# Moving the last recurrent groups of two batches behind the MLP's 64-feature products

## The chip, the cores and the metric

One core of a Trainium2 chip runs the whole kernel. The metric is the device time of one execution in microseconds. The kernel before took 391.72 us (median of three runs, 391.14 to 392.08). Engines are called as in the profile: PE (TensorE, matmuls), PEld (its weight loads), DVE (VectorE), ACT (ScalarE), POOL (GpSimd), SP (which issues the DMAs).

## The reference

An mLSTM cell over 4 batches, 8 heads, 768 tokens and a head size of 40 is followed by a Fourier mix with an MLP on the 320 features of each token. Cut to what is computed:

```
for t in range(S):                                   # mLSTM, per batch and head
    m_new  = max(f[t] + m, i[t])
    f_stab, i_stab = exp(f[t] + m - m_new), exp(i[t] - m_new)
    C = f_stab * C + i_stab * outer(v[t], k[t])
    n = f_stab * n + i_stab * k[t]
    y[t] = sigmoid(o[t]) * (C @ q[t]) / max(abs(n @ q[t]), 1)
x  = y as (batch, 768, 320)
u  = x + real(fft(fft(x, axis=1), axis=2))
un = (u - mean(u)) / sqrt(var(u) + 1e-6)
out = u + relu(un @ w_ch1) @ w_ch2                   # w_ch1 320x1280, w_ch2 1280x320
```

## The kernel before

Batches are counted from 1 to 4 in the text (0 to 3 in the code), chunks of 128 tokens from 0 to 5. A batch passes three stages: the recurrence (mLSTM), the mix (two Fourier steps as matmuls over folded tokens), and the MLP. The stages of neighbouring batches are interleaved: while TensorE works on the MLP of one batch, the recurrence of the next runs between its matmuls.

The order is written out by hand. `at(slot, phase, fn, ...)` puts a step into a plan; `run` calls the steps sorted by slot and then by phase (EVAC 0, FILL 1, MAIN 2, FILL_PE 3), and each engine executes its instructions in the order in which they were issued. An engine that waits for a semaphore holds up all that stands behind it in its queue.

**The recurrence of batches 2 to 4** (`plan_halves`, L762) takes each chunk in halves of 64 tokens, with 64-row and 64-column matmuls. Chunk c has a start slot s, before always three slots after the last. Steps at s: scores (L626) and the new state (L637) on TensorE, exponentials on ScalarE (L491, four at slot s-1 and four at s), decay, scaling and mask on GpSimd (L652, L507, L501, L515), state adds and weighing on DVE (L667, L672). Three slots later comes the output: the part from the state (L674), the part from the chunk in two turns (L685), between which ScalarE reads one element (`halves_between`, L699) so that the second turn waits for the first, and a tanh (L605). All these matmuls have line L519. The output tile `ph` is a single one (`heads`), as are the scores. One slot later `mlstm_finish` (L712 to L720, five DVE operations) reads `ph` and writes the chunk's x; the chunks 0, 1 and 3 run backwards in time order and are then moved by DMAs (`halves_rows`, L728). For the last chunk (`end`) the state part and the first turn stand ahead of the slot's MLP step, the second turn behind it.

**The mix** folds pairs of chunks on DVE (`mix_fold`, L815 to L827, pairs (2,3), (1,4), (0,5) at slots x_done), then the folded rows once more in three steps (`mix_fold_again`, L844 to L854).

**The MLP of batches 2 to 4** (`plan_mlp`, L1271) computes its first layer in five blocks of four slots. A block (`mlp_block`, L1111) multiplies by the first and the last 128 features in a scheme with seven products for eight; each product is a 128x128 by 128x384 matmul in fp32 (L1121). The 64 features between are four matmuls on 64 rows (`tails`, L1126), two at a time on the two halves of the array's rows. Product by product, with the lines of the operands:

- slot 0: in block 0 a first product B (`begin`, L1138, copied out by ScalarE, L1139); then A01 (L1146)
- slot 1: S2 (L1152, copied out, L1153, into h12) and A10 (L1151 or L1155, added to h12 by DVE, L1130)
- slot 2: S4 (L1160), S3 (L1161, copied out, L1162), then the four tails, and DVE adds three banks to the hidden values (L1165 to L1167, all in line L1130)
- slot 3: B of the next block, and T4 (L1172), with a relu on ScalarE (L1173)

The second tail adds into the bank that DVE's add of A10 has read; the fourth into the bank that ScalarE's copy of S3 (L1162) has read; B of the next block writes the bank that the first of DVE's three adds reads. The sums of inputs that the scheme needs are four DVE subtractions per batch (`mlp_sums`, L1109) just before block 0: A10 of block 0 reads the second one's result, S2 the third's. The second layer (`mlp_out_pair`, L1240) follows the blocks.

The MLP of batch 2 has its blocks at slots 63 to 82, that of batch 3 at 95 to 114. The recurrence of batch 3 starts at slot 53 and that of batch 4 at slot 83. In the line for the sixth argument of `plan_mix`, `done` holds the slots at which the folds become possible:

```
done = [s_mlstm + n for n in ((16, 19, 22) if b == 0 else (18, 21, 22))]
```

Of the kernel before, what the change touches and what calls it, by code (L numbers as in the profile page):

```python
# [53 lines left out]
def kernel(  # L54
# [33 lines left out]
    def bank(name, shape, n=None):  # L88

        return ps_m.tile(shape, FP, name=name, tag=f"pm{next(turn) if n is None else n}")  # L90
# [33 lines left out]
    def at(slot, phase, fn, *args):  # L124
        plan.setdefault((slot, phase), []).append((fn, args))
# [7 lines left out]
    EVAC, FILL, MAIN, FILL_PE = range(4)  # L133
# [625 lines left out]
            at(t, FILL_PE + (2.5 if c < 4 else 1), mlstm_turn, b, c, c < 4)  # L759
            at(x, FILL + 0.05, mlstm_finish, b, c)  # L760

    def plan_halves(b, s0, stride=3):  # L762
        for c in range(NT):
            s = s0 + stride * c
            t = 22 + 2 * c if b == 1 and c < 3 else s - 5
            at(t, FILL, mlstm_load, b, c)
            at(t, FILL, mlstm_load_max, b, c)
            at(34 if b == 1 and c == 2 else t + 1, FILL, mlstm_load_decay, b, c)
            at(s - 1, FILL, mlstm_load_o, b, c)
            at(s - 1, FILL, mlstm_scale_v, b, c)  # L770
            at(s - 1, FILL + 0.3, mlstm_exp, b, c, 0)
            at(s, FILL, mlstm_exp, b, c, NP)
            at(s, FILL_PE + 2.05, halves_scores, b, c)
            at(s, FILL_PE + 2.5, halves_to_state, b, c)
            for i in range(2):
                at(s + i, FILL + 0.05, halves_decay, b, c, i)
                at(s + 1 + i, FILL - 0.2, halves_add, b, c, i)
            at(s, FILL + 0.1, mlstm_scale_q, b, c)
            at(s + 1, FILL, mlstm_mask, b, c)
            if (b, c) == (3, 2):  # L780
                at(s + 2, MAIN + 0.1, halves_weigh, b, c)
            else:
                at(s + 1, FILL + 0.55 if b == 1 and c > 0 else MAIN + 0.7, halves_weigh, b, c)
            end = c == NT - 1
            at(s + 3, MAIN - 0.1 if end else FILL_PE, halves_from_state, b, c)
            at(s + 3, MAIN - 0.1 if end else FILL_PE, halves_from_chunk, b, c, 0)
            at(s + 3, MAIN if end else FILL_PE + 0.5, halves_between, b, c)
            at(s + 3, FILL_PE + 3, halves_from_chunk, b, c, 1)
            at(s + 3, FILL_PE + 0.6, mlstm_tanh, b, c)
            at(s + (5 if (b, c) == (2, 2) else 4), {(2, 4): FILL + 0.3, (3, 3): FILL - 0.3}.get((b, c), FILL + 0.3 if b == 1 else MAIN + 0.55), mlstm_finish, b, c)  # L790
            at(s + 6, FILL - 0.6, halves_rows, b, c)

# [215 lines left out]
    def plan_mix(b, s0, x_done, s_feat, s_add, s_turn):  # L1010
        for j in range(TG):
            p = TG - 1 - j
            at(x_done[j] + (b > 1 and j == TG - 1), FILL + 0.5 if b < 2 else FILL_PE + 0.2, mix_fold, b, p)
            if b == 0:
                at((s0 - 4, s0 - 2, s0)[j], FILL_PE + 4, mix_seq, b, p, (0, 1))
                at((s0 - 2, s0 - 2, s0)[j], FILL_PE + 4, mix_tail, b, p)
            elif b == 1 or j == 0:
                if b > 1:
                    for step, slot in enumerate((x_done[0], x_done[-1] + 2, x_done[-1] + 6)):
                        at(slot, FILL_PE + 0.25, mix_fold_again, b, step)  # L1020
                at(s0, FILL_PE + 4, mix_seq, b, p, (0,))
                at(s0 + 1, FILL_PE + 4, mix_seq, b, p, (1,))
                at(s0 + 2, FILL_PE + 4, mix_tail, b, p)
        for i in range(2):
            at(s0 + 1 if b == 0 else s0 + 1 + i, FILL, mix_seq_out, b, i)
        at(s0 + (1 if b == 0 else 3), FILL + 0.1, mix_tail_out, b)
        for p in range(TG):
            at(s_feat[p], FILL_PE + 4, mix_feat, b, p)
        for c, a, t in zip(ORDER, s_add, s_turn):
            at(a, FILL if b < 2 else MAIN - 0.3 if c == 0 else MAIN + 0.5, mix_add, b, c)  # L1030
            at(t, FILL + 0.1, mix_center, b, c)
            at(t, FILL_PE + (5 if b == 0 or c in ORDER[:4] else -0.1), mix_turn, b, c)
            if b > 0:
                at(t, FILL_PE + 6, mix_turn_out, b, c)
            elif t < s_mlp:
                at(t + 1, FILL + 0.2, mix_turn_out, b, c)
            else:
                at(t + 1, EVAC, mix_turn_out, b, c)
# [31 lines left out]
    def hidden(gr, f):  # L1070
        return hid[gr, f % 2][:, f // 2 * TG * L:(f // 2 + 1) * TG * L]
# [7 lines left out]
    def block(t, n):  # L1079
        return t[:, n * L:(n + 1) * L]  # L1080
# [20 lines left out]
    def mlp_u(gr, ch):  # L1101
        return uT_bufs[gr][:, ch].rearrange("p c t -> p (c t)")
# [8 lines left out]
    def mlp_block(b, i, step):  # L1111

        k = mixes[b]
        f = 2 * i
        T2, T3, T4 = w1x["T"]
        A = {(r, ch): block(w1_sb[:, ch], f + r) for r in range(2) for ch in range(2)}

        def product(bank, w, u, start=False):  # L1120
            nc.tensor.matmul(bank, w, u, start=start, stop=True, skip_group_check=True)  # L1121

        def tails(gr, banks):
            for r, bank in enumerate(banks):
                rows = slice(r * TAIL, (r + 1) * TAIL)
                nc.tensor.matmul(bank, block(w1t_sb, i)[rows], mlp_u(gr, 1)[rows], start=False, stop=True,  # L1126
                                 skip_group_check=True)

        def add(h, bank):
            nc.vector.tensor_tensor(out=h, in0=h, in1=bank, op=OP.add)  # L1130

        banks = list(range(4) if i % 2 else range(3, -1, -1))

        def begin(i):


            k.p1 = bank("pm", [L, TG * L], 0 if i % 2 else 3)
            product(k.p1, block(w1_sb[:, 0], 2 * i), mlp_u(0, 0), True)  # L1138
            nc.scalar.copy(out=hidden(0, 2 * i), in_=k.p1)  # L1139

        (h11, h21), (h12, h22) = ([hidden(gr, f + r) for r in range(2)] for gr in range(2))
        if step == 0:
            if i == 0:
                begin(0)
            k.pm = [k.p1, bank("pm", [L, TG * L], banks[1])]
            product(k.pm[1], A[0, 1], mlp_u(0, 2), True)  # L1146
        elif step == 1:
            k.pm.append(bank("pm", [L, TG * L], banks[2]))
            p1, _, p5 = k.pm
            if i == 0:  # L1150
                product(p5, A[1, 0], mlp_u(1, 0), True)  # L1151
            product(p1, block(w1x["S2"], i), T2)  # L1152
            nc.scalar.copy(out=h12, in_=p1)  # L1153
            if i > 0:
                product(p5, A[1, 0], mlp_u(1, 0), True)  # L1155
            add(h12, p5)
        elif step == 2:
            k.pm.append(bank("pm", [L, TG * L], banks[3]))
            p1, p2, p5, p3 = k.pm
            product(p3, block(w1x["S4"], i), mlp_u(1, 2), True)  # L1160
            product(p1, block(w1x["S3"], i), T3)  # L1161
            nc.scalar.copy(out=h22, in_=p1)  # L1162
            tails(1, (p3, p5))
            tails(0, (p2, p1))
            add(h12, p3)  # L1165
            add(h22, p5)
            add(h11, p2)  # L1167
        else:
            p1 = k.p1
            if i < NFF // 2 - 1:  # L1170
                begin(i + 1)
            product(p1, A[1, 1], T4)  # L1172
            nc.scalar.activation(out=h21, in_=p1, func=AF.Relu, scale=-1.0)  # L1173
# [97 lines left out]
    def plan_mlp(b, s):  # L1271
        groups = range(NT // TG)
        for i in range(NFF // 2) if b > 0 else ():
            for step in range(4):
                at(s, MAIN, mlp_block, b, i, step)
                s += 1
            end = i == NFF // 2 - 1
            for n, (gr, f) in enumerate(((1, 2 * i + 1), (1, 2 * i), (0, 2 * i))):
                at(*((s - 1, MAIN + (-0.1 if gr else 0.1)) if end else (s + n, MAIN + 0.5)), mlp_relu_in_place, gr, f)
# [31 lines left out]

    def plan_batch(b, s_mlstm, s_mix, s_mlp):
        (plan_halves if b > 0 else plan_mlstm)(b, s_mlstm)
        done = [s_mlstm + n for n in ((16, 19, 22) if b == 0 else (18, 21, 22))]
        assert s_mix >= done[-1] and s_mlp >= s_mix + 9
        late = [s_mlp + 2 * c for c in range(TG)]
        if b == 0:
# [13 lines left out]
        s = s_mlp + NFF + 2  # L1331
# [4 lines left out]

    s_mlp = 31
    plan_batch(0, 0, 22, s_mlp)
    plan_batch(1, 32, 54, s_mlp + MLP_SLOTS)
    plan_batch(2, 53, 83, s_mlp + 2 * MLP_SLOTS)  # L1340
    plan_batch(3, 83, 115, s_mlp + 3 * MLP_SLOTS)
    for n in range(4):
# [149 lines left out]
```

## Time and profile before

The profiled execution took 392.19 us, of which the span of the engines' work is 390.4 us.

| | us or count |
|---|---|
| profiled execution, its span | 392.19, 390.4 |
| median of the runs | 391.72 |
| ACT busy, POOL busy | 172.1 (44%), 134.9 (35%) |
| L519 groups of the recurrence, one whole group in the MLP | 1.9 us |
| L1126 MATMUL, mean of one | 508 ns |
| L1121 MATMUL, mean of one (two records a product) | 506 ns |
| L1130 DVE add of a bank, mean of one | 548 ns |
| mean granted clock of TensorE | 0.999 |

A line of the trace in order of time gives start, duration, engine, line, operation, the tiles written and read, and how many instructions are merged; in brackets stands how long the engine was idle before and who released it. As matmuls overlap in the pipe, distances from start to start say more than durations. A product of fp32 shows as two records. The chain of waits gives, in order of time, what the end depended on.

### The profile page before, as it was taken

The page shows a single profiled execution, that of the slowest core. Times are in us where ns is not written, and L with a number is a line of the kernel's source. Part 1 is how long each engine was busy: PE and PEld are TensorE (multiplying, and loading weights), DVE is VectorE, ACT ScalarE, POOL GpSimd, SP SyncE. Part 2 cuts the span into 40 slices and gives each one's busy share as a digit, 9 for nine tenths or more (in the row PEclk, how much of TensorE's full clock was granted, in tenths as well). Part 3 has the DMA queues.
Part 4 walks back from the last instruction along what each step waited for, and adds up shares of the span by engine and source line. Part 5 has one row for each costly group of instructions (what it writes and reads, how often), then busy time and mean ns, then how long its engine had stood idle before and what let it go on. Part 6 is the DMA issues. An engine that isn't in the chain of part 4 may idle for free.

```text
span 390.4 us, 10585 instructions
## 1 busy us (share of the span) xinstructions
PE 379.6 (97%) x4174; PEld 277.3 (71%) x4174; DVE 278.0 (71%) x671; ACT 172.1 (44%) x481; POOL 134.9 (35%) x237
## 2 busy tenths in 40 slices
PE   8999899999999999999999999999999999999996
PEld 6777555656667777765569998755588996556996
DVE  7789988499599587476975699777655785346652
ACT  6887357477543233655462314554530133545000
POOL 5739504467954442173254134541500000020000
PEclk9999999999999999999999999999999999999999
DMA  7887499579394345437700626400000000000101
GB/s 224 287 235 204 159 254 255 179 214 271 109 231 116 122 116 150 149 102 184 182 2 28 174 80 192 135 20 2 0 2 34 6 30 34 2 0 0 35 34 35
DMA packets 25631, 44.78 MB, mean 115 GB/s; under 512 B 5727, under 2 KB 14766, under 8 KB 25454
## 3 DMA queue, kind: packets, MB, share of 16 engines
q1 hardware_dynamic: 25582, 44.11, 38.9%
q8 instruction: 33, 0.54, 0.6%
q14 instruction: 16, 0.13, 0.1%
HBM read 38.49 MB, written 4.12 MB: 109 GB/s over the span
## 4 chain that ended last, share of the span: by engine, by line
PE 78%; DVE 14%; issue 3%; ACT 3%; POOL 1%; DVEq 0%; ACTq 0%; POOLq 0%
PE po L1240 20%; PE pm L1121 15%; PE po L1184 8%; PE pm L1059 7%; PE ph L519 4%; PE pm L1126 4%; PE pu L938 4%; PE ps L519 3%; PE pm L1050 2%; PE put L981 2%; PE pz L907 1%; PE pz L895 1%; DVE h L1130 1%; DVE so L716 1%; PE pM L221 1%
## 5 line engine op out<-in xcount | busy, mean ns | idle before, releaser
L1190 DVE SCALAR_TENSOR_TENSOR x<-po,rstd,x 128x160 f32<-128x160 f32 (+1 forms) x69 | 27.1, 394 | 37.4 <-PE po L1240 32.5
L1130 DVE TENSOR_TENSOR h<-h,pm 128x384 f32<-128x384 f32 x60 | 30.5, 548 | 27.1 <-PE pm L1121 12.6
L652 POOL TENSOR_TENSOR C<-C,decB 128x164 f32<-128x164 f32 x30 | 15.9, 531 | 67.5 <-DVE C L667 56.1
L1121 PE MATMUL pm<-uT,w_sb 128*128 128x384 f32 x90 | 37.7, 506 | 1.3 <-DVE uT L1109 0.6
L491 ACT ACTIVATE W<-W,colT 128x64 f32<-128x64 f32 x144 | 37.5, 339 | 0.4 <-DMA W<-M_d 0.4
L1184 PE MATMUL po<-w_sb,h 128*128 128x320 f32 x120 | 34.3, 435 | 0.0
L515 POOL TENSOR_SCALAR_AFFINE_SELECT W<-W 64x512 f32<-64x512 f32 x36 | 27.3, 759 | 10.6 <-ACT W L491 9.1
L1005 POOL TENSOR_TENSOR t<-rstd 128x6 f32<-128x6 f32 x12 | 3.3, 273 | 79.9 <-DVE v L999 79.4
L1059 PE MATMUL pm<-uT,w_sb 128*128 128x384 f32 x80 | 29.2, 500 | 0.1
L1184 PEld LDWEIGHTS po<-w_sb,h 128*128 128x128 f32 x120 | 22.3, 190 | 9.5 <-issue 0.6
L1240 PE MATMUL po<-T,S 128*128 128x160 f32 x180 | 27.8, 301 | 0.3 <-DVE x L1190 0.3
L501 POOL TENSOR_TENSOR qg<-qk,Gb 128x512 f32<-128x512 f32 (+1 forms) x21 | 27.1, 1290 | 1.7 <-DMA qk<-in_qkT 1.6
L1240 PEld LDWEIGHTS po<-T,S 128*128 128x128 f32 x180 | 25.5, 190 | 1.7 <-DVE x L1190 0.5
L1121 PEld LDWEIGHTS pm<-uT,w_sb 128*128 128x128 f32 x90 | 15.5, 189 | 15.6 <-DVE h L1130 6.7
L1240 PE MATMUL po<-w_sb,h 128*128 128x160 f32 x180 | 26.3, 300 | 0.0
L1240 PEld LDWEIGHTS po<-w_sb,h 128*128 128x128 f32 x180 | 25.2, 190 | 1.4 <-DVE x L1190 0.3
L986 ACT COPY uT<-put 128x384 f32<-128x384 f32 x24 | 11.2, 477 | 30.1 <-PE put L981 30.1
L507 POOL TENSOR_TENSOR vw<-kvt,colT 128x328 f32<-128x328 f32 x23 | 19.7, 859 | 13.1 <-DMA qk<-in_qkT 10.1
L1177 ACT ACTIVATE h<-h 128x384 f32<-128x384 f32 x45 | 23.1, 520 | 2.0 <-DVE h L1130 2.0
L1126 PE MATMUL pm<-uT,w1t_sb 64*128 64x384 f32 x120 | 23.4, 508 | 0.0
L1059 PEld LDWEIGHTS pm<-uT,w_sb 128*128 128x128 f32 x80 | 14.1, 189 | 9.6 <-issue 1.9
L974 ACT ACTIVATE uc<-x 128x384 f32<-128x384 f32 x24 | 14.4, 613 | 12.6 <-DVE x L966 11.1
(241 smaller groups left out, 843.4 us busy)
## 6 DMA issues: line engine op xcount, KB each, us to landing
kvt<-in_kv SPq DMA_DIRECT2D x24, 336.0 KB
qk<-in_qkT SPq DMA_DIRECT2D x48, 160.0 KB
raw<-in_w SPq DMA_DIRECT2D x10, 640.0 KB
Gb<-G_d SPq DMA_DIRECT2D x36, 128.0 KB
W<-M_d SPq DMA_DIRECT2D x36, 128.0 KB
so<-in_o SPq DMA_DIRECT2D x24, 160.0 KB
out<-x SPq DMA_DIRECT2D x24, 160.0 KB
x<-so SPq DMA_DIRECT2D x9, 140.0 KB
```

Source lines behind the costliest of these rows:

```text
L491: nc.scalar.activation(out=k.W[:, h, :], in_=M, func=AF.Exp, scale=-1.0, bias=colT[:, c, 0, b * H + h:b * H + h + 1])
L501: nc.gpsimd.tensor_tensor(out=k.qg[:, :, t], in0=k.qk[:, 0, :, t], in1=k.Gb[:, :, t], op=OP.mult)
L515: nc.gpsimd.affine_select(out=W, in_=W, compare_op=OP.is_ge, fill=0.0, base=base, pattern=[[0, H], [step, LH]], channel_multiplier=-1)
L519: nc.tensor.matmul(out, w, x, start=start, stop=True, skip_group_check=True)
L1059: nc.tensor.matmul(k.pm[i], w1_sb[:, ch, f0:f0 + L], u[2 * ch], start=(ch == 0 and not ahead), stop=(ch == 1 and ahead), skip_group_check= ...
L1121: nc.tensor.matmul(bank, w, u, start=start, stop=True, skip_group_check=True)
L1126: nc.tensor.matmul(bank, block(w1t_sb, i)[rows], mlp_u(gr, 1)[rows], start=False, stop=True, skip_group_check=True)
L1130: nc.vector.tensor_tensor(out=h, in0=h, in1=bank, op=OP.add)
L1177: nc.scalar.activation(out=h, in_=h, func=AF.Relu, scale=-1.0)
L1184: nc.tensor.matmul(k.po[gr, i], hidden(gr, f)[:, i * L:(i + 1) * L], w2_sb[:, f, :], start=(f == 0), stop=(f == NFF - 1))
L1190: nc.vector.scalar_tensor_tensor(out=u, in0=po, scalar=k.rstd[:, c:c + 1], in1=u, op0=OP.mult, op1=OP.add)
L1240: nc.tensor.matmul(po, a[:, f], w[:, f], start=start and f == 0, stop=f == half - 1, skip_group_check=True)
```

## The change

Chunks keep a list of start slots instead of a stride of three. For batch 2 the list is the old one. For batch 3 chunk 5 starts at 69 (before 68), and the outputs of chunks 4 and 5 come at 69 and 73 (before 68 and 71). For batch 4 chunks 4 and 5 start at 97 and 101 (before 95 and 98), and the outputs of chunks 3, 4 and 5 come at 97, 101 and 105 (before 95, 98 and 101). These are the slots of the tails. Everything that hangs on a chunk's start (loads, exponentials, scores, new state) or on its output (finish, row moves) moves with it. The tails and their three adds become a step of their own in the same slot, slightly later in phase, and the last chunk's state part and first turn come between S3 and the tails. In batch 4 the folds come two slots later, the second step of the second folding two slots later, its third step one slot later.

In the order of instructions that results, TensorE has the four tails ahead of the groups of chunks 3 (batch 4) and 4 (both), and for chunk 5 the state part and first turn ahead of the tails and the second turn behind them. On DVE the finish of each of these chunks now stands behind the three adds of its block. On ScalarE, the second four exponentials of chunk 5 stand ahead of the copy L1162. On GpSimd the scaling of v (L507) of chunk 4 of batch 4 goes behind two copies of one row. On SP, loads, row moves and output stores change places. The new file has one more line above `mlp_block`'s lines and two more within it.

```diff
-    def plan_halves(b, s0, stride=3):
+    def plan_halves(b, s0):
+        starts = [s0 + n for n in ((0, 3, 6, 9, 12, 15, 18), (0, 3, 6, 9, 12, 16, 20), (0, 3, 6, 9, 14, 18, 22))[b - 1]]
         for c in range(NT):
-            s = s0 + stride * c
+            s, o = starts[c:c + 2]
...
-            at(s + 3, MAIN - 0.1 if end else FILL_PE, halves_from_state, b, c)
-            at(s + 3, MAIN - 0.1 if end else FILL_PE, halves_from_chunk, b, c, 0)
-            at(s + 3, MAIN if end else FILL_PE + 0.5, halves_between, b, c)
-            at(s + 3, FILL_PE + 3, halves_from_chunk, b, c, 1)
-            at(s + 3, FILL_PE + 0.6, mlstm_tanh, b, c)
-            at(s + (5 if (b, c) == (2, 2) else 4), {(2, 4): FILL + 0.3, (3, 3): FILL - 0.3}.get((b, c), FILL + 0.3 if b == 1 else MAIN + 0.55), mlstm_finish, b, c)
-            at(s + 6, FILL - 0.6, halves_rows, b, c)
+            at(o, (MAIN - 0.1 if b == 1 else MAIN + 0.02) if end else FILL_PE, halves_from_state, b, c)
+            at(o, (MAIN - 0.1 if b == 1 else MAIN + 0.02) if end else FILL_PE, halves_from_chunk, b, c, 0)
+            at(o, (MAIN if b == 1 else MAIN + 0.03) if end else FILL_PE + 0.5, halves_between, b, c)
+            at(o, FILL_PE + 3, halves_from_chunk, b, c, 1)
+            at(o, FILL_PE + 0.6, mlstm_tanh, b, c)
+            at(o + (2 if (b, c) == (2, 2) else 1), {(2, 4): FILL + 0.3, (3, 3): FILL - 0.3}.get((b, c), FILL + 0.3 if b == 1 else MAIN + 0.55), mlstm_finish, b, c)
+            at(o + 3, FILL - 0.6, halves_rows, b, c)
...
-                    for step, slot in enumerate((x_done[0], x_done[-1] + 2, x_done[-1] + 6)):
+                    for step, slot in enumerate((x_done[0], x_done[-1] + 2, x_done[-1] + (6 if b == 2 else 5))):
...
             nc.scalar.copy(out=h22, in_=p1)
+        elif step == 3:
+            p1, p2, p5, p3 = k.pm
             tails(1, (p3, p5))
             tails(0, (p2, p1))
             add(h12, p3)
...
-            for step in range(4):
-                at(s, MAIN, mlp_block, b, i, step)
-                s += 1
+            for step in range(5):
+                at(s, MAIN + 0.05 * (step == 3), mlp_block, b, i, step)
+                s += step != 2
...
-        done = [s_mlstm + n for n in ((16, 19, 22) if b == 0 else (18, 21, 22))]
+        done = [s_mlstm + n for n in ((16, 19, 22) if b == 0 else (20, 23, 24) if b == 3 else (18, 21, 22))]
```

## The prediction

> **What bounds the kernel now.** I read the page first (shares, clock, chain), then TensorE in order of time around the two stretches that the change touches (163 to 201 us, where the MLP of batch 2 hosts the recurrence of batch 3, and 248 to 286 us, MLP of batch 3 with recurrence of batch 4), then VectorE, ScalarE and GpSimd in the same windows, and last the chain of waits through both.
>
> ```profile
> PE 379.6 (97%) x4174; PEld 277.3 (71%) x4174; DVE 278.0 (71%) x671; ACT 172.1 (44%) x481; POOL 134.9 (35%) x237
> PE 78%; DVE 14%; issue 3%; ACT 3%; POOL 1%; DVEq 0%; ACTq 0%; POOLq 0%
> ```
>
> TensorE is busy 97% of the span, but 14% of the ending chain is VectorE: there are places where TensorE runs only as fast as VectorE lets it. TensorE in order of time, batch 3:
>
> ```profile
> 174.16 0.81 PE L1121 MATMUL pm<-uT,w_sb 128*128 128x384 f32 x2
> 174.90 0.68 PE L519 MATMUL ph<-C,qg 40*64 40x41 f32 x32
> ...
> 176.75 0.44 PE L519 MATMUL ph<-kvt,W 64*64 64x41 f32 x16 [0.30 <-ACT warm L699]
> 177.12 0.91 PE L1121 MATMUL pm<-uT,raw 128*128 128x384 f32 x2
> 177.87 0.81 PE L1121 MATMUL pm<-e,raw 128*128 128x384 f32 x2
> 178.61 1.56 PE L1126 MATMUL pm<-uT,w1t_sb 64*128 64x384 f32 x8
> 180.17 0.91 PE L1121 MATMUL pm<-uT,w_sb 128*128 128x384 f32 x2
> ```
>
> Read start to start: a full product is 0.645 us when a full product follows (173.52 to 174.16), but 0.74 before a small group (174.16 to 174.90) and 0.75 as the first after one (177.12 to 177.87). This is what the change attacks. The chain of waits, a little later:
>
> ```profile
> 183.78 1.50 PE pm L1121 x4
> 185.33 0.04 issue
> 185.37 0.56 DVE h L1130
> ...
> 193.25 0.41 DVE eo L827
> 193.69 0.08 DVE fe L822
> 193.77 0.16 issue
> 193.93 0.56 DVE h L1130
> 194.53 4.78 PE pm L1121 x14
> ```
>
> From 185.37 to 194.5 the chain is VectorE without a break: its queue (bank adds, finishing of the last chunk, folds, weight sums) already sets when block 4 of this MLP begins. And batch 4's start, TensorE and then VectorE:
>
> ```profile
> 249.78 0.68 PE L519 MATMUL ph<-C,qg 40*64 40x41 f32 x32
> ...
> 252.08 0.91 PE L1121 MATMUL pm<-uT,w_sb 128*128 128x384 f32 x2 [0.35 <-DVE uT L1109]
> 253.00 0.91 PE L1121 MATMUL pm<-raw 128*128 128x384 f32 x2
> ```
>
> ```profile
> 249.65 0.81 DVE L1109 TENSOR_TENSOR e<-uT 128x384 f32<-128x384 f32 x1
> 250.50 1.53 DVE L1109 TENSOR_TENSOR uT<-uT,uT 128x384 f32<-128x384 f32 x1
> 252.06 0.88 DVE L1109 TENSOR_TENSOR raw<-uT 128x384 f32<-128x384 f32 x1
> ```
>
> Even with a recurrent group in front, TensorE waits here for VectorE's second subtraction, and then for the third.
>
> **What the Trainium skill says.** TensorEngine Tiling (Array Packing), Key Properties: changing the tiling mode drains TensorE. It gives no price; the trace agrees with the 0.10 us on each side above. SBUF — State Buffer, Who interferes with whom: a VectorE instruction with two SBUF inputs and a GpSimd instruction that reads SBUF exclude each other, and whichever issued first holds on. The trace agrees: the three subtractions above ran beside GpSimd's decay, qg product and mask; the same ones a batch earlier, with GpSimd idle, took 0.56 each (163.87 to 165.6). TensorE: Matmul & The Clock Gate, What's actually happening: an idle window of about 3.4 us halves the clock. No gap here is that long; the granted clock is 0.999.
>
> **The change part by part.** Batches are 1 to 4, chunks 0 to 5. I name the products of MLP block i by their place: B (begun in the block before), A01, A10, S2, S4, S3, the four 64-feature tails, next B, T4. In block 0 the order is B, A01, A10, S2.
>
> *Price of one merged visit.* Alone, a group costs 0.10 (product before) + 0.12 (its last turn takes 0.35 to a full product, 0.23 to another group) + 0.10 (product after); the tails cost 0.10 + 0.06 (1.55 to a full product, 1.49 to a group, 168.11 to 169.60) + 0.10. Together 0.58; merged 0.32. Saved: 0.26 a visit. Three visits of each batch merge (batch 3: chunk 5's scores with chunk 4's output, and the two parts of chunk 5's output; batch 4: chunk 3's, chunk 4's and the first part of chunk 5's). About 1.6 us in all, if nothing else moved.
>
> *Batch 3.* Up to A10 of block 1 (174.16) nothing changes. Then S4 174.81, S3 175.45, tails 176.19. ScalarE's order in the build now has the second four exponentials ahead of the copy that frees S3's bank: T4's relu and another to 173.95, four exponentials (1.05), copy, relu, four exponentials to 176.85, copy to 177.28. The fourth tail, which normally starts some 0.75 into the tails, waits 0.39. Group at 176.19 + 1.49 + 0.39 = 178.07. It takes 1.71 (as 258.68 to 260.39; the 0.30 wait goes), so block 2 begins at 179.78, before 180.17. To the end of S3 0.75 + 5 x 0.645 + 0.74 = 4.71, then state part 0.49 and first turn 0.23: tails of block 2 at 185.21, before 186.49. So far 1.28 gained.
>
> Now VectorE. Before, chunk 5's finish ran ahead of these tails' adds. Now its output ends after the tails, so it queues behind the adds, and VectorE idles before them. The queue from 0.95 after the tails' start (186.16): three adds 1.40, finish 1.59, fold 1.59, L1212 0.90, the four small rstd steps 0.56, add 0.47, fold 1.59, add 0.51 = 8.61, to 194.77. Rows: 187.43 to 188.83, 185.84 to 187.43, 188.83 to 190.42, to 191.32, to 191.88, to 192.34, to 193.93, 194.44. On the way block 3's second tail waits about 1 us for the add at 192.1 to 192.6, and block 4's B, which needs the last add's bank, starts at 194.86 (0.09 after), before 194.53. The gain is gone: **+0.33**.
>
> *Batch 4, block 0.* Chunk 3's group leaves 249.78. VectorE's queue up to the subtractions is unchanged in the built order, so A10, which would be ready at 249.7, stands until the second subtraction: that moves 2.0 us from work to waiting (idle 2.3 instead of 0.35). GpSimd now runs vw (0.74), decay (0.46) and qg (1.26) beside the three, no longer the mask. Taking turns from 249.62: vw to 250.36, first subtraction to 250.92, decay 251.38, second 251.94, qg 253.20, third 253.76. If VectorE's third goes before qg it ends at 252.5. This is the largest unknown; I take the third at 253.2, A10 at 252.0, S2 at 253.25. S3 follows 1.48 later as now (253.00 to 254.48, the ScalarE copy between), tails 255.47, chunk 3's group 256.96 for 1.88 (169.60 to 171.48), block 1's B at 258.84. Before 257.20, of which 0.31 was a wait for an add that goes.
>
> *Blocks 1 to 4.* 4.71 to the tails at 263.55, fourth tail late by 0.45 behind the exponentials as in batch 3, group 265.49, block 2's B at 267.26 (before 266.92, since two merged groups no longer stand between). 4.71 + 0.72: tails of block 2 at 272.69, before 271.63. VectorE's queue is the same without L1212: 0.95 + 7.71 + 0.09 = 8.75, block 4's B at 281.44, before 279.55: **+1.89**. VectorE then still has its folding sums done by some 287, and the seq products of batch 4 come near 291, so the moved fold step costs nothing.
>
> *Edits without cost.* SP issues c4's and c5's loads, o gates and row moves later and in another order, two stores of outputs go ahead of loads; the loads are still issued five slots ahead (the last near 256 us, wanted at 261), and the folds' row moves, issued at 260 to 262, are wanted at 269. On GpSimd one vw moves behind the two row copies, counted above. The drop in batch 4's last fold step from 6 to 5 slots places it at slot 112. If the loads came late, the exponentials would hold ScalarE and the tails with it.
>
> *Sum.* +0.33 + 1.89 = +2.2 us. The profiled execution was 392.19 (span 390.4 and 1.8 around it), so it would be 394.4; on the median 391.72 the forecast is 393.9.
>
> **Rivals.**
> - *VectorE's subtractions run at their own 0.56.* Then the second ends at 250.8, the third at 251.4; S2 at 251.45 instead of 253.25, 1.8 less: +0.4, 392.1. For it: the rows of 163.87. Against: GpSimd has 2.46 us of work that reads SBUF from 249.6 on.
> - *Faster: the array change costs more than the starts show.* If one merged visit saves y, the sum is 2.2 - 6(y - 0.26); it is zero at y = 0.63, and at 0.83 the time is 390.5. For it: ends of matmuls are modelled, so hidden drain may sit inside the groups. Against: the single product between two groups (182.49 to 183.34) takes 0.85, only 0.2 over 0.645.
> - *Clock.* The 2.3 us gap could lie so that the gate closes; half speed for one window of 3.4 us costs 1.7 more: 395.6. Against: no gap under 3.4 us did so in this trace.
> - *The build doesn't follow the slots:* excluded, its order has the groups behind the tails on TensorE.
>
> **How the numbers follow.** Forecast 0.64, subtractions 0.16, faster 0.13, clock 0.07. Own range of the forecast: both waits behind exponentials gone (0.84 less) and the third subtraction early (0.6 less) give +0.8; the third late (0.5) and 0.3 for an entry from a group to the tails, which no row shows, give +3.0. Range 391.6 to 395.0, leaving out the faster and the clock case. 0.2% is 0.78 us, about what a measurement of this kernel tells from no change: faster 0.13, same 0.16 (the subtraction case), slower 0.71.
>
> **What would show it.** After: no lone L519 group between full products at 174 to 184 and 257 to 264; a TensorE gap of about 2 us before the first A10 of batch 4, released by uT L1109; VectorE idle some 2 us ahead of block 2's adds in both batches, then unbroken to block 4's B; ScalarE's h copy (L1162 before) behind exponentials. Wrong if block 4 of batch 3's MLP begins over a microsecond earlier relative to its block 1, or if that gap is under 1 us.

## The result, and the profile after

The changed kernel takes 394.56 us (median of six executions, 393.30 to 395.72), the kernel before 391.74 in the same session (391.14 to 392.08): a ratio of 1.0070, with a 95% interval of 1.0056 to 1.0085. It is slower by 2.8 us; forecast were 393.9 us, 2.2 more than before, and a range of 391.6 to 395.0. The execution that the profile shows is the longest of the six, 395.72 us with a span of 394.0; part of its length is a clock that another execution does not have, as will be seen.

Lines in the new file stand one further on up to L1163 (before L1162) and three further on behind it. The shares and the ending chain of the page after:

```profile
PE 379.8 (96%) x4174; PEld 277.6 (70%) x4174; DVE 279.9 (71%) x671; ACT 172.3 (44%) x481; POOL 133.8 (34%) x237
PE 78%; DVE 14%; issue 3%; DMA 2%; ACT 2%; SPq 1%; DVEq 0%
```

The number of instructions is the same on every engine, the span is 3.6 us longer. A page of sums does not say where; the two stretches do. TensorE after in order of time, MLP of batch 2 (start, duration, operation, tiles, merged records, idle before):

```profile
163.40 2.57 PE L1122 MATMUL pm<-uT,w_sb 128*128 128x384 f32 x6
...
176.12 1.80 PE L1127 MATMUL pm<-uT,w1t_sb 64*128 64x384 f32 x8
177.85 0.68 PE L519 MATMUL ph<-C,qg 40*64 40x41 f32 x32
...
184.27 0.68 PE L519 MATMUL ph<-C,qg 40*64 40x41 f32 x32
...
185.11 1.56 PE L1127 MATMUL pm<-uT,w1t_sb 64*128 64x384 f32 x8
...
191.69 2.61 PE L1127 MATMUL pm<-uT,w1t_sb 64*128 64x384 f32 x8
194.79 0.91 PE L1122 MATMUL pm<-uT,w_sb 128*128 128x384 f32 x2 [0.50 <-DVE h L1131]
```

The same places before (the last line is block 0 of the MLP of batch 3):

```profile
163.48 2.57 PE L1121 MATMUL pm<-uT,w_sb 128*128 128x384 f32 x6
...
192.75 1.56 PE L1126 MATMUL pm<-uT,w1t_sb 64*128 64x384 f32 x8
194.53 0.91 PE L1121 MATMUL pm<-uT,w_sb 128*128 128x384 f32 x2 [0.21 <-DVE h L1130]
...
248.40 1.45 PE L1121 MATMUL pm<-uT,w_sb 128*128 128x384 f32 x4
```

The change does what its words say: the groups (L519) follow the tails (L1127) directly. Block 2's tails begin 21.71 us after block 0 (163.40 to 185.11), before 23.01 (163.48 to 186.49), so 1.30 us are gained. Ten microseconds later nothing of it is left. The tails of block 3 take 2.61 instead of 1.56, and block 4 stands 0.50 for an add (before 0.21). The chain of waits after says for whom:

```profile
190.76 0.90 DVE w_sb L1215
...
192.23 0.45 DVE h L1131
...
194.19 0.56 DVE h L1131
```

The add at 192.23 holds the second tail of block 3, that at 194.19 block 4. Both stand in VectorE's queue behind finish, folds and the weight sum L1215, and VectorE could begin that queue only when the tails of block 2 had been computed. It idled 1.93 us ahead of their adds:

```profile
186.06 1.48 DVE L1131 TENSOR_TENSOR h<-h,pm 128x384 f32<-128x384 f32 x3 [1.93 <-PE pm L1127]
```

From block 0 to block 4 this MLP takes 31.39 us (163.40 to 194.79), before 31.05.

TensorE after, MLP of batch 3:

```profile
248.67 1.45 PE L1122 MATMUL pm<-uT,w_sb 128*128 128x384 f32 x4
251.80 0.91 PE L1122 MATMUL pm<-uT,w_sb 128*128 128x384 f32 x2 [1.67 <-DVE uT L1110]
253.43 1.53 PE L1122 MATMUL pm<-raw 128*128 128x384 f32 x2 [0.72 <-DVE raw L1110]
254.75 1.49 PE L1122 MATMUL pm<-uT,raw 128*128 128x384 f32 x2
256.03 1.26 PE L1122 MATMUL pm<-e,raw 128*128 128x384 f32 x2
257.22 1.56 PE L1127 MATMUL pm<-uT,w1t_sb 64*128 64x384 f32 x8
...
283.08 0.91 PE L1122 MATMUL pm<-uT,w_sb 128*128 128x384 f32 x2 [0.50 <-DVE h L1131]
```

The recurrent group that used to fill the time until the second subtraction is gone, so TensorE stands 1.67 us ahead of A10, and 0.72 ahead of S2 for the third. VectorE and then GpSimd in the same window, in order of time:

```profile
249.92 1.08 DVE L1110 TENSOR_TENSOR e<-uT 128x384 f32<-128x384 f32 x1
251.04 0.70 DVE L1110 TENSOR_TENSOR uT<-uT,uT 128x384 f32<-128x384 f32 x1
251.78 1.50 DVE L1110 TENSOR_TENSOR raw<-uT 128x384 f32<-128x384 f32 x1
```

```profile
249.86 0.73 POOL L507 TENSOR_TENSOR vw<-kvt,colT 128x328 f32<-128x328 f32 x1
250.56 0.77 POOL L652 TENSOR_TENSOR C<-C,decB 128x164 f32<-128x164 f32 x1
251.29 1.58 POOL L501 TENSOR_TENSOR qg<-qk,Gb 128x512 f32<-128x512 f32 x1
```

The two engines take turns, as the Trainium skill has it (SBUF — State Buffer, Who interferes with whom): the subtractions take 0.56 each a batch earlier, without GpSimd, and 1.08, 0.70 and 1.50 beside it. The ends alternate between GpSimd and VectorE: 250.59, 251.00, 251.33, 251.74, 252.87, 253.28. Each step from end to end is 0.13 to 0.15 shorter than the instruction that ends it takes alone (0.56 for a subtraction, 0.46 for decay, 1.26 for qg).

Then comes what the sum had not counted: the three products from S2 on take 1.32, 1.28 and 1.19 us from start to start, where the kernel before has 0.75, 0.73 and 0.85. The granted clock by stretches of time, core 0 after (stretch; its length; busy time and count of PE, PEld, DVE, ACT, POOL; clock, DMA):

```profile
251.00:254.00 3.00, 1.48 (x3) 0.71 (x4) 2.21 (x3) 0.00 (x0) 1.87 (x2) 0.92 0.60 183
254.00:258.00 4.00, 4.00 (x12) 1.93 (x12) 1.02 (x2) 1.92 (x6) 1.31 (x2) 0.63 0.87 209
```

Before, both stretches have 1.00. Cut more finely, the clock of this execution is 0.50 from 253.52 to 256.94, for 3.42 us, and 1.00 on both sides. In the 3.40 us ahead of that, TensorE was busy for 1.01 us. So this execution lost about 1.5 us to the clock, and the MLP takes 34.41 us from block 0 to block 4 (248.67 to 283.08) instead of 31.15 (248.40 to 279.55): 1.8 of the 3.26 are the waits, 1.5 the clock.

### The profile page after: what moved, and what is told of

Its sections match the earlier page's. It is cut to its first block, busy times and chain, and to the rows that moved or that the text cites. A ratio compares the mean times of both kernels' runs of the same rounds, so it can differ in the third digit from the quotient of the medians.

```text
span 394.0 us, 10579 instructions
## 1 busy us (share of the span) xinstructions
PE 379.8 (96%) x4174; PEld 277.6 (70%) x4174; DVE 279.9 (71%) x671; ACT 172.3 (44%) x481; POOL 133.8 (34%) x237
## 4 chain that ended last, share of the span: by engine, by line
PE 78%; DVE 14%; issue 3%; DMA 2%; ACT 2%; SPq 1%; DVEq 0%
PE po L1243 19%; PE pm L1122 16%; PE po L1187 8%; PE pm L1060 6%; PE pm L1127 5%; PE ph L519 4%; PE pu L939 4%; PE ps L519 3%; DMA kvt<-in_kv 2%; PE pm L1051 2%; PE put L982 2%; DVE so L716 2%; PE pz L896 1%; PE pz L908 1%; PE pi L139 1%
## 5 line engine op out<-in xcount | busy, mean ns | idle before, releaser
L1243 PE MATMUL po<-T,S 128*128 128x160 f32 x180 | 27.8, 301 | 0.3 <-DVE x L1193 0.3
L1243 PEld LDWEIGHTS po<-T,S 128*128 128x128 f32 x180 | 25.5, 190 | 1.7 <-DVE x L1193 0.5
L1243 PE MATMUL po<-w_sb,h 128*128 128x160 f32 x180 | 26.3, 300 | 0.0
L1243 PEld LDWEIGHTS po<-w_sb,h 128*128 128x128 f32 x180 | 25.2, 190 | 1.4 <-DVE x L1193 0.3
L1127 PE MATMUL pm<-uT,w1t_sb 64*128 64x384 f32 x120 | 24.9, 511 | 0.1
L507 POOL TENSOR_TENSOR vw<-kvt,colT 128x328 f32<-128x328 f32 x23 | 18.9, 822 | 13.4 <-DVE colT L360 10.9
L1127 PEld LDWEIGHTS pm<-uT,w1t_sb 64*128 64x128 f32 x120 | 12.4, 185 | 10.9 <-issue 7.4
```

The costliest lines, as they stand in the source:

```text
L1243: nc.tensor.matmul(po, a[:, f], w[:, f], start=start and f == 0, stop=f == half - 1, skip_group_check=True)
```

## The experiments

All compare with the kernel before, run on the same chip at the same time. "Low clock" counts the executions whose mean granted clock over the whole span is under 0.998; they stand at 0.994 to 0.996, all others at 0.999 or 1.000. A row that begins with "and" adds an edit to the row above it. The last two kernels ran on another chip than the other experiments.

| kernel | median us (lowest to highest, n) | ratio and interval | low clock |
|---|---|---|---|
| after | 394.56 (393.30 to 395.72, 6) | 1.0070 [1.0056, 1.0085] | 2 of 6 |
| after, again | 394.12 (393.07 to 397.97, 20) | 1.0067 [1.0048, 1.0085] | 4 of 20 |
| batch 3 alone | 392.08 (391.07 to 393.72, 14) | 1.0007 [0.9996, 1.0018] | 0 of 14 |
| batch 4 alone | 393.62 (392.77 to 396.49, 9) | 1.0059 [1.0037, 1.0082] | 2 of 9 |
| chunk 3 back | 392.12 (391.56 to 393.12, 14) | 1.0009 [1.0000, 1.0019] | 0 of 14 |
| gap filled | 394.17 (393.32 to 394.88, 6) | 1.0056 [1.0039, 1.0073] | 0 of 6 |
| queue | 393.68 (391.81 to 395.07, 22) | 1.0044 [1.0029, 1.0060] | 12 of 22 |
| queue and chunk 3 back | 391.12 (390.45 to 393.18, 21) | 0.9978 [0.9964, 0.9991] | 0 of 21 |
| and exponentials | 390.70 (389.75 to 390.93, 21) | 0.9964 [0.9951, 0.9977] | 0 of 21 |
| and fold step | 389.83 (388.95 to 390.17, 6) | 0.9939 [0.9925, 0.9954] | 0 of 6 |
| queue and fold step | 392.88 (392.06 to 393.79, 11) | 1.0024 [1.0012, 1.0036] | 8 of 11 |

**Which batch costs?** *Batch 3 alone* keeps only the part of the change that concerns batch 3:

```diff
-(0, 3, 6, 9, 12, 16, 20), (0, 3, 6, 9, 14, 18, 22))[b - 1]
+(0, 3, 6, 9, 12, 16, 20), (0, 3, 6, 9, 12, 15, 18))[b - 1]
...
-(20, 23, 24) if b == 3 else (18, 21, 22)
+(18, 21, 22)
```

> Only batch 3's groups move; batch 4 keeps its old slots, folds and phases. Theory (VectorE's queue and the first gap of batch 4): TensorE gains about 1.3 us up to block 2's tails in batch 3 and loses it again before block 4, +0.3 us in all, 392.0; no gap over 1 us at 248 to 254. Rival (each merged visit costs by itself, half of the loss in each batch): +1.4 us, 393.1.

*Batch 4 alone* keeps the other part:

```diff
-(0, 3, 6, 9, 12, 16, 20), (0, 3, 6, 9, 14, 18, 22))[b - 1]
+(0, 3, 6, 9, 12, 15, 18), (0, 3, 6, 9, 14, 18, 22))[b - 1]
```

> Only batch 4's groups move; batch 3 keeps its old slots and phases. Theory: nearly the whole loss, 394.2 (393.2 where the clock stays full, 395.3 where it drops), with the gap before the second subtraction's reader. Rival (loss by visits): +1.4 us, 393.1.

In both, the phases of the last chunk's output follow the batch. Measured: 392.08 and 393.62. TensorE with batch 3 alone, block 3's tails and block 4:

```profile
190.50 2.61 PE L1127 MATMUL pm<-uT,w1t_sb 64*128 64x384 f32 x8
193.60 0.91 PE L1122 MATMUL pm<-uT,w_sb 128*128 128x384 f32 x2 [0.50 <-DVE h L1131]
```

The same two waits, and 31.38 us from block 0 to block 4: batch 3's merged visits are worth nothing at the end of the stretch. With batch 4 alone, block 0 and block 4 of its stretch, at full clock:

```profile
247.55 1.45 PE L1122 MATMUL pm<-uT,w_sb 128*128 128x384 f32 x4
...
280.46 0.91 PE L1122 MATMUL pm<-uT,w_sb 128*128 128x384 f32 x2 [0.50 <-DVE h L1131]
```

The distance is 32.91, 1.76 more than before. The ratios, 0.07% and 0.59%, add up to 0.66%, the changed kernel's 0.67 to 0.70%. The cost is batch 4's.

**Is it the gap ahead of A10?** *Chunk 3 back* puts the output of batch 4's chunk 3 and the start of its chunk 4 back where they were, into the gap; the other two visits of batch 4 stay merged:

```diff
-(0, 3, 6, 9, 14, 18, 22)
+(0, 3, 6, 9, 12, 18, 22)
```

> The change, but chunk 3 of batch 4 puts its output back into block 0 after the first two products (slot 95), and chunk 4 starts there; chunks 4 and 5 stay at 101 and 105. Theory: the gap shrinks to about 0.4 us and the clock stays full, but VectorE's queue before block 4 still takes the gains of both batches: 392.2. Rival (the gap is the only fault): gains of 1.3 and 0.7 us stay, 389.7.

```profile
252.51 0.91 PE L1122 MATMUL pm<-uT,w_sb 128*128 128x384 f32 x2 [0.33 <-DVE uT L1110]
253.43 0.91 PE L1122 MATMUL pm<-raw 128*128 128x384 f32 x2
...
280.10 0.91 PE L1122 MATMUL pm<-uT,w_sb 128*128 128x384 f32 x2 [0.50 <-DVE h L1131]
```

In TensorE's order of time the wait ahead of A10 is 0.33, that ahead of S2 is gone, and block 4 begins 31.26 us after block 0 (before 31.15). The time is 392.12. So nearly all of the change's loss is this one group in the wrong place. And with two merged visits left in batch 4, block 4 still begins no earlier: it waits 0.50 for VectorE's add, as in batch 3.

**What is the clock's part?** *After, again* runs the changed kernel unchanged, for more executions.

> The changed kernel once more, for the share of executions with a clock drop. Theory: two groups of times, one near 393.7 and, in about a third of the runs, one near 395.6. Rival (no groups, only a wider spread): times spread evenly from 393 to 396.

By time alone the 20 executions spread without a clean break, so the two groups that were expected do not stand out, and the share at low clock is a fifth, not a third. By their clock they part better: the 16 at full clock have a median of 394.0 us (393.07 to 395.74), the four at low clock one of 395.5 us (394.99 to 397.97). The spread of 2.7 us at full clock stays unexplained. The profile of one at full clock, TensorE:

```profile
250.87 0.91 PE L1122 MATMUL pm<-uT,w_sb 128*128 128x384 f32 x2 [1.67 <-DVE uT L1110]
252.50 0.88 PE L1122 MATMUL pm<-raw 128*128 128x384 f32 x2 [0.72 <-DVE raw L1110]
253.22 0.81 PE L1122 MATMUL pm<-uT,raw 128*128 128x384 f32 x2
253.95 0.91 PE L1122 MATMUL pm<-e,raw 128*128 128x384 f32 x2
...
280.66 0.91 PE L1122 MATMUL pm<-uT,w_sb 128*128 128x384 f32 x2 [0.50 <-DVE h L1131]
```

The gaps are the same to the hundredth as in the first profile of the changed kernel, but the products behind them follow in 0.72 and 0.73 us. The same gaps cost the clock in one execution and not in the next.

*Gap filled* leaves the change as it is, but gives TensorE four small products (128x128 by 128x256) ahead of A10 of batch 4's block 0; their result is overwritten:

```diff
             if i == 0:
+                if b == 3 - 1:
+                    for _ in range(4):
+                        nc.tensor.matmul(p5[:, 0:2 * L], rest[:, 0:L], rest, start=True, stop=True, ...)
```

> The change with four additional 128x256 matmuls on zeros (about 0.43 us each) in the gap before the first A10 of batch 4, into the bank that A10 starts afresh; results unchanged. Theory (the idle gap lets the clock drop in a part of the executions): the wait for VectorE remains, the clock stays full, 393.5 with all runs within about 1 us. Rival (the drop has another cause, or the matmuls lengthen the path): 394.6 or more, spread of 2.4 us as before.

```profile
250.13 1.89 PE L1154 MATMUL pm<-rest 128*128 128x256 f32 x8
251.96 0.91 PE L1122 MATMUL pm<-uT,w_sb 128*128 128x384 f32 x2
253.60 0.88 PE L1122 MATMUL pm<-raw 128*128 128x384 f32 x2 [0.72 <-DVE raw L1110]
254.32 0.81 PE L1122 MATMUL pm<-uT,raw 128*128 128x384 f32 x2
```

The time lost to the subtractions stays (32.92 us from block 0 to block 4), and none of the six executions is at low clock. Their median, 394.17, is 0.7 above what was expected and close to that of the changed kernel's executions at full clock. Six executions are few: with 6 of 26 at low clock without the filling, none of six comes by chance about one time in five.

Over all kernels: with the open gap 28 of 68 executions are at low clock, with the gap closed or filled none of 82. (The kernel before had one, 396.15, among 73 in one session, and none in the others.) The clearest pair are *queue* and *queue and chunk 3 back*, below: they differ in the one number that puts chunk 3's output and chunk 4's start into the gap, and have 12 of 22 and none of 21. So the low clock belongs to the open gap, and in the two profiled executions that have it (the first of the changed kernel and that of *queue and fold step*) it is one stretch at 0.50, of 3.42 and 3.40 us, that begins in the second gap or just behind it, with 1.00 in every other ten microseconds up to 380. That it is the idle time that does it, and not the place of the group, rests on the six filled executions and is not settled. Nor is what decides which executions lose it: with the reordered queue it is 20 of 33, without it 8 of 35, although the gaps are the same.

**Is VectorE's queue what keeps batch 3 from gaining?** *Queue* takes the changed kernel and reorders VectorE around block 4 of the MLPs of batches 2 and 3: the last fold goes behind block 3's adds, the weight sum (L1215) and the four rstd steps behind block 3's add of A10, the second step of the second folding one slot later.

```diff
-at(x_done[j] + (b > 1 and j == TG - 1), ..., mix_fold, b, p)
+at(x_done[j] + 3 * (b > 1 and j == TG - 1), ..., mix_fold, b, p)
...
-(x_done[0], x_done[-1] + 2, x_done[-1] + (6 if b == 2 else 5))
+(x_done[0], x_done[-1] + 3, x_done[-1] + (6 if b == 2 else 5))
...
-        at(s, FILL + 0.6, mix_rstd, b)
+        at(s + 1 if b > 0 else s, FILL_PE + 0.1 if b > 0 else FILL + 0.6, mix_rstd, b)
-            at(s + 3 * n if b == 0 else s, FILL + 0.65, mix_rstd_step, b)
+            at(s + 3 * n if b == 0 else s + 1, FILL + 0.65 if b == 0 else FILL_PE + 0.15, mix_rstd_step, b)
...
-        at((56, 57, 58, 75)[n], FILL + 0.4, out_weight_sums, n)
+        at((56, 57, 58, 76)[n], FILL_PE if n == 3 else FILL + 0.4, out_weight_sums, n)
```

> The change with VectorE's queue reordered in both batches: block 3's add of A10 ahead of the output weights' sum and the rstd steps, and block 3's three adds ahead of the last fold. Theory: the wait inside block 3's tails (1.1 us in batch 3, 0.2 in batch 4) and the wait before block 4's B (0.5 each) go, 2.3 us in all, while the gap of batch 4 and its clock drops stay: 392.2, a few runs near 394. Rival (the queue is late as a whole, the wait moves to a later add or to the mix): 393.5 or more.

*Queue and chunk 3 back* adds the list with chunk 3 back:

> The queue reordered, and chunk 3 of batch 4 back in block 0. Theory: the two faults add up, so 392.1 less 2.3 us: 389.8, 2 us below before. Rival (merged visits gain nothing, only the lost time comes back): 391.7, as before.

Both missed: 393.68 instead of 392.2, where the rival had 393.5 or more, and 391.12 instead of 389.8. The mechanism was there, in batch 3. TensorE with both edits:

```profile
191.76 1.56 PE L1127 MATMUL pm<-uT,w1t_sb 64*128 64x384 f32 x8
193.31 0.91 PE L1122 MATMUL pm<-uT,w_sb 128*128 128x384 f32 x2
```

The tails take their 1.56 again, block 4 waits for nobody, and block 0 to block 4 takes 29.83 us, 1.22 less than before. In batch 4 that distance fell too, from 31.15 to 30.62, but what follows did not come earlier. VectorE and TensorE of the same kernel at the end of batch 4's block 4:

```profile
283.41 0.56 DVE L854 TENSOR_TENSOR fe<-fe 128x384 f32<-128x384 f32 x1 [0.94 <-POOL fe L852]
...
284.95 1.47 DVE L1131 TENSOR_TENSOR h<-h,pm 128x384 f32<-128x384 f32 x3
```

```profile
285.55 2.98 PE L1243 MATMUL po<-w_sb,h 128*128 128x160 f32 x20 [0.61 <-DVE h L1131]
```

L854, the third step of the second folding, waits for four small GpSimd steps that its second step (now later) sets off. Block 4's three adds stand behind it, and the second layer (L1243) waits for one of them. It begins 38.35 us after block 0, before 38.10: the gain was spent at the next hand-over.

*And exponentials* adds to that kernel that the second four exponentials of chunk 5 go behind ScalarE's copy that frees S3's bank:

```diff
-at(s, FILL, mlstm_exp, b, c, NP)
+at(s, MAIN + 0.01 if b > 1 and c == NT - 1 else FILL, mlstm_exp, b, c, NP)
```

> As the last one, and the second four exponentials of chunk 5 stand behind ScalarE's copy of S3 in batches 3 and 4. Theory: the fourth tail no longer waits 0.24 us in either batch: 389.3, tails of block 1 of 1.49 us instead of 1.73. Rival (the mask and the weighing of chunk 5 then come late and hold the output): 390 or more.

Block 1's tails now last 1.49 to the group in both batches, so the wait of 0.24 is gone twice. The median fell by 0.42, which by itself is not clear of the spread. The level was missed, since it had been set before L854's wait was found. The rival's number came true, but not for its reason: no wait of TensorE was added behind block 1, and the 0.61 ahead of the second layer is as before this edit. The next two kernels move L854 behind the three adds:

```diff
-x_done[-1] + (6 if b == 2 else 5)
+x_done[-1] + 6
```

*And fold step* does so on top of all the edits above:

> The run before with one more edit: the third step of batch 4's second folding stands six slots after the last fold, as in batch 3, so that VectorE's add L854 comes behind block 4's three adds. In the run before, VectorE stood 0.94 us ahead of that add, waiting for GpSimd's L852, and the three adds behind it ended so late that the second layer waited 0.61 us for one of them. Theory (this wait is what swallowed the gain in batch 4): the three adds come 1.4 us earlier, the second layer starts 0.7 earlier without a wait, and the time is 390.0, 0.7 below the run before. Rival (the last folded rows are the tighter deadline): the seq products then wait for the add and for GpSimd's copy behind it, and the time stays at 390.5 or above.

VectorE, then TensorE:

```profile
283.20 1.47 DVE L1131 TENSOR_TENSOR h<-h,pm 128x384 f32<-128x384 f32 x3
284.60 0.55 DVE L854 TENSOR_TENSOR fe<-fe 128x384 f32<-128x384 f32 x1
```

```profile
284.04 2.88 PE L1243 MATMUL po<-w_sb,h 128*128 128x160 f32 x20
```

No wait is left at either place, and the second layer begins 37.33 us after block 0. With 29.60 us in batch 3's stretch that is 1.45 + 0.77 = 2.2 us less than before. Measured: 389.83, 0.9939 of the kernel before with an interval of 0.9925 to 0.9954, faster than both.

*Queue and fold step* has the changed kernel's slots, gap included, with the reordered queue and the moved L854:

> The run with the changed kernel's slots and the reordered VectorE queue, with the same edit: L854 behind block 4's adds. Theory: what that run fell short by was this wait, 0.7 us; the time is 393.0. Rival (something else limits that queue): 393.6, no different from the run without the edit.

Measured 392.88. Here too the clock has to be kept apart: at full clock the median of *queue* is 392.7 (10 executions) and of this kernel 392.1 (3), at low clock 394.2 (12) and 393.2 (8). With so few executions, on two chips, L854's wait comes out at 0.6 to 1.0. The traces of *and exponentials* and *and fold step* put it at 0.8, by the start of the second layer after block 0 (38.12 and 37.33). The first miss, 393.68 for 392.2, was this wait and the low clock together.

## Why the prediction was right

**Merged visits save 0.26 us each.** Confirmed. From block 0 to block 3 of batch 3's stretch 0.99 us is gained. A wait for ScalarE that is gone gives 0.47 of it (176.12 to 176.75 before, 179.06 to 179.22 after), the fourth tail takes back 0.24, and 0.76 are left for three visits. The start of block 2's tails fits even better (21.71 us after block 0, expected 21.73), but with some luck: the fourth tail waits 0.15 less than expected, and the last chunk's state part and first turn take 0.84 ahead of the tails (184.27 to 185.11) and not 0.72.

**The fourth tail waits for the copy behind the exponentials.** Confirmed in place, too large in size: 0.24 in each batch (1.73 for 1.49) instead of 0.39 and 0.45.

**Batch 3: VectorE's queue takes the gain back, +0.33.** Confirmed: 31.39 for 31.05, so +0.34, with the second tail of block 3 waiting about 1 us, as worked out. That the queue is the cause is shown by its reordering, which turned +0.34 into -1.22 (29.83).

**Batch 4: A10 waits for the second subtraction, S2 for the third, +1.89.** Confirmed: +1.76 at full clock. Counted from block 0's start in each, A10 was expected after 3.60 us and came after 3.13 (A10 at 251.80, 0.2 earlier than forecast, while block 0 had begun 0.27 later), but S2, which decides, after 4.76 (expected 4.85). Reckoned as the forecast did it, from where the product would have followed the one before, A10 stands 1.8 and not 2.3 us. Taking turns with GpSimd, the largest unknown, was met in part by luck. The third subtraction was put at 253.2, between 252.5 and 253.76 for the two possible orders, and ended at 253.28. The order that came is the slower one; it ended before 253.76, though it began 0.3 late, because the turns are shorter than the instructions alone. The small remainder of 0.13 has its terms too: 0.21 less for the fourth tail's wait and 0.06 from a slip in the sum (265.49 + 1.71 is 267.20, not 267.26), against 0.12 more for the state part and first turn. The rival with 0.56 for each is ruled out by the rows.

**Clock, chance 0.07.** Not an alternative to the forecast but a part of it: 6 of 26 executions of the changed kernel are at low clock, which cost 1.5 us in the profiled one, where 1.7 was the estimate from the skill's window length. The prediction leaned on there being no idle window of about 3.4 us, from the Trainium skill (TensorE: Matmul & The Clock Gate, What's actually happening). The length agrees with the stretches at half clock, 3.42 and 3.40 us. But the time ahead of them need not be idle throughout: gaps of 1.67 and 0.72 us with one product between were enough, and TensorE was busy for 1.01 and 1.47 of the 3.40 us ahead. The same section says that the window runs free of the program and that the point of transition shifts from run to run, which would fit the measured "sometimes"; no run here tests it. At full clock the changed kernel's median is 394.0 over 20 executions, the forecast 393.9; the rest of 394.56 is the low clock and the chance of six executions.

**Faster, if the array change costs more than the starts show.** Ruled out: three visits brought 0.76 us, 0.25 each, and what they brought ended at VectorE's queue.

**Edits without cost.** They held: in the stretches of the change no exponential waits for a load, and L854 in the changed kernel follows the add ahead of it without a gap (287.15 behind 286.68). The statement holds for this queue alone: with the queue shortened, the same step 5 slots after the last fold cost about 0.8 us.

## What to carry to other kernels

A small group of matmuls that costs array changes may be the one that covers a wait; before moving it, look at what the next product would wait for without it. A gain on TensorE ahead of a queue that another engine works off without a break is lost at the end of that queue, so the queue has to be reordered in the same edit, and the next hand-over looked at too. Of two places where work could be merged, keep the merge that leaves no idle time on TensorE, since an open gap can cost twice: once itself, once in the clock behind it.

## What the runs showed of the hardware

- Kernels with idle stretches of 1.67 and 0.72 us on TensorE, separated by one product, had a mean granted clock of 0.994 to 0.996 in 28 of 68 executions, kernels with these gaps closed or filled in none of 82. In the two such executions with a profile, the clock was 0.50 for 3.42 and 3.40 us from the second gap on and 1.00 before and after it, and products of 0.73 to 0.75 us took 1.3 to 1.4.
- Four products on data of no use, which fill the first gap, left no execution of six at low clock, too few to be sure. They did not move the product behind the gap: A10 starts 3.12 us after block 0's start with them, 3.13 without.
- VectorE subtractions of 128x384 with both inputs in SBUF and GpSimd products took turns: 0.56 us alone became 1.08, 0.70 and 1.50, with each turn 0.13 to 0.15 us shorter than the instruction alone.
- A visit to 64-row matmuls between products on 128 rows cost 0.25 us less when merged with another such visit (0.76 us for three).
